# Casting loads for most of block 0, one-hot rows copied by engines, bounds from three products, and a new order table, in a fused attention and softplus kernel

## The chip, the cores and the metric

The kernel runs on one core of a Trainium2 chip. The metric is the device time of one execution in microseconds (us). Engines are named as in the profile: PE is the matrix engine, DVE the vector engine, ACT the scalar engine, POOL the GpSimd engine, SP the engine whose queue issues transfers. POOL issues transfers too.

## The reference

Two layers. The first is attention over 4 batches, 8 heads, 768 positions, 64 dimensions, in which each query sees only six chunks of 32 keys: those with the largest upper bound on the score.

```
k_min = min of k over each chunk of 32;  k_max = max
ub   = sum over d of max(q * k_min, q * k_max)        # one bound per query and chunk
ub   = where(query chunk >= key chunk, ub, -1e9)
top  = the 6 chunks with the largest ub
scores = q @ k.T / 8, kept where the chunk is in top and the key is not later than the query
attn = softmax(scores) @ v
```

The second layer takes the 3072 rows of attn (512 wide): `h = x @ w_in` (512 x 2048), `g = max(h, 0) + log1p(exp(-|h|))`, that is ln(1 + exp(h)), and `out = g @ w_out` (2048 x 512). Inputs and output are float32.

## The kernel before

The work is cut into 12 blocks: 4 batches by 3 stretches of 256 queries. For each block n the program makes operations with short names, which the order table and this text use:

- `ld k n`, `ld q n`, `ld v n`: loads into a bfloat16 buffer (tile io; v for values), two for each, `.0` and `.1`. For n > 0 they are casting transfers (float32 in memory, bfloat16 on chip) that POOL issues. For block 0 q and k come as float32 by SP's queue into tile wx (`load_pairs`), in halves of four heads, and an operation `cast` on ACT or DVE makes bfloat16 of each.
- `kT`, `qT`: transposes on PE (with the matrix ident), for blocks 0 to 2; later blocks use transposing transfers `kD`, `qD`.
- `kx`, `kn`: maxima and negated minima of k by chunk (DVE, two reductions). `bd`: these, copied into a block-diagonal tile BD. `kc`: keys copied into tiles ka and kb. `qc`: queries copied into tile qt; `qac`: a second copy into tile qa.
- `qpn`: the positive part of q and the positive part of -q (tiles qpos, qneg). `ub`: products of these with BD, which give the bound, and for blocks 0 to 2 a product with constants (rows4, neg4) that puts later chunks out.
- `mx`: the largest six (DVE); `raw`: which chunks are out; `mT`: that matrix transposed on PE (blocks 0 to 2), or by a transfer `mD` (later); `mc`: the result copied under q, so that the score product adds a large negative number to what is out. For this the key tiles hold one-hot rows: `oh` makes them, `ohk` are transfers on SP's queue that put them into ka and kb.
- `s`: scores (PE); `ex`: exp (ACT); `af`: the causal edge (POOL); `av`: the product with v (PE); `nm`: division (DVE); `oT`, `xc`: transpose and copy into x (blocks 0 to 2), `xD` later.
- `h`: eight matmuls with w_in for two of 16 column tiles of the second layer; `e`, `ln`: exp and ln(1 + .) on ACT; `y`: products with w_out; `ye`: eviction; `st`: the store.

Block 0 does its attention's front end in two groups of four heads (g0, g1), so `kT0`, `kx0`, `mx0` and the like occur twice or more.

Nothing is scheduled at run time. A string, ORDER, names every operation once, with a letter for the engine (P, A, V, G, S for PE, ACT, DVE, POOL, SP) and `#i` for the i-th operation of that name. Each engine runs its operations in that order, and one waits for what it depends on and for free buffers. A word `z12` puts matmuls on a zero tile there, worth 12 units of 128 columns: four units make one matmul of 512 columns, the rest are matmuls of 128. They compute nothing that is used; this text calls them dummies.

Of the kernel before, what the change touches and what calls it, by code (L numbers as in the profile page):

```python
# [12 lines left out]
ALU = mybir.AluOpType  # L13
# [7 lines left out]
NP = H // 2  # L21
# [124 lines left out]
def dve(n, rate=1.0):  # L146
# [47 lines left out]
    sizes=dict(s=2, h=2, y=1, o=1, t=2, xp=4, kT=2, io=8, kx=2, q=2, pn=1, ub=2, pt=4, osw=2, x=3, g=2, e=3, ysb=4,  # L194
# [7 lines left out]
Vzero Sld_k0.0 Acast_k0.0 Vmr0#1 Vkb0 Vmr0 Gvone Gident z32 PkT0 PkT0 Sld_q0.0 Vr4 Gc4 Vbd0 Vkx0 Vkn0 Sld_k0.1  # L202
Vcast_k0.1 Acast_q0.0 z6 PqT0 PqT0 Aqc0 Vbd0#2 Gld_k1.0 Gld_k1.1 Vqpn0 Aqpn0 Sld_q0.1 Acast_q0.1 z36 PqT0 Gld_q1.0
Gld_q1.1 PkT1 Vcm0 Voh Akc0 Akc0 PkT0 PkT0 Sohk Sohk#3 Sohk PqT0 Vkx0 Vkn0 Aqc0 Aqpn0#3 z5 PkT1 Pub0 Gld_q2.0 Aqpn0
Akc0#3 Vmx0 Vraw0 Gqac0#1 Gbd0#3 Gqac0 Gld_v0.0 Gld_v0.1 Vkx1 Sohk z28 PmT0 PqT1 PqT1 Amc0 Aqc1 Vkn1 Vbd1 Vkc1 z16
Ps0#2 z5 Pub0 Ps0 Vmx0 Vqpn1 Vraw0 z35 PmT0 Vqac1 Amc0 Aqpn1 Pub1 Aex0#2 Aex0 Akc0 Vmc0#3 Gld_k2.0 Gld_k2.1 Vmc0 z7
Ps0#4 Ps0 Aex0 Gld_q2.1 Gld_v1.0 Aex0#4 Gld_v1.1 Gaf0 z12 Ps0#5 Aex0#5 Vmx1 Vraw1 z3 Ps0 Gaf0 Aex0 Pav0 z3 Pav0 Gaf0
Gw_in0 Vnm0 Gaf0 PqT2 Gw_in1 Gld_q3.0 Ps0#7 PmT1 Vmc1 Gw_in2 Akc1 z4 PoT0 Ps0 Aex0 Aex0 z12 Ps1#12 Pav0 Pav0 Aex1#12
Axc0 PkT2 PkT2 Ps1#4 Vmc1 Gaf0#6 Gaf0 Gaf0 Aex1#4 Vnm0 Gaf0 Gld_k3.0 z3 PqT2 Ps1#5 Aex1#5 PoT0 z1 Ps1#7 z5 Ps1 Gcm z10
Pav0#6 Pav0#7 Gvone Vkx2 Vkn2 Vnm0#3 Axc0 Aqc2 Aex1#7 Aex1 z7 Ps1 Aex1 z3 Pav0 Vbd2 Vqpn2 Vqpn2 Ps1#3 Aex1#3 Gaf1#1  # L210
PoT0#3 z1 Ps1 z4 Ps1#15 Pav0 Vnm0 Vkc2 Vqac2 Aex1 Gaf1 z4 Ps1#8 Pub2 Axc0#3 Aex1#15 Ps1#11 Aex1#8 Aex1#11 Gw_in3 PoT0
Ps1#13 Pav1 z3 Ps1#9 Pav1 Gld_k3.1 Aex1#13 Gw_out0 Gaf1#6 Gaf1 Ps1#14 Axc0 Vmx2 Gaf1#7 Vraw2 Aex1#9 Aex1#14 Ph0 Ps1#10
Aex1#10 Ps1 Vnm1 Gaf1 Aex1 Ae0 Gaf1 Gld_q3.1 PmT2 Vmc2 Ph0 Gaf1 Pav1#6 Pav1#7 Vnm1#3 Vkc2 Ps2#6 Ae0 Gld_v2.0 Aex2#6
Ps2#8 Aex2#8 Ph0#3 Aln0 Ps2#2 Pav1 Pav1 Ps2 Aex2 Ph0 SkD3 Vnm1 Vmc2 Ps2#12 Pav1 Pav1 Aex2#2 PoT1 Vxc1 Ae0 Vnm1 Ps2#5
Vbd0 PoT1 Ph0 Aex2#12 Aex2#5 Ae0 Ps2#17 PoT1 Ps2#14 Aex2#17 Vxc1 Vxc1 Ph0 PoT1 Vxc1 Ps2 Aex2#14 Ae0 Ps2#9 Ae0 Aex2 Ph0
Ps2#11 Aex2#9 Gaf2 Aex2#11 Ae0 Gw_out1 Ph0 Ae0 Ps2 Ps2 Gaf2#4 Gaf2#2 Ph1 Gaf2#5 Ph1#2 Gld_v2.1 Vkx3 Aex2 Aex2 Ps2#18
Aln0 Gaf2 Pav2 Ps2 Gwh0 Gw_out2 Vkn3 Vbd3 Gw_out3 Aex2#18 Py0 Aex2 Ae1 Ps2 Aln0 Aex2 Ps2#22 Ph1 Ae1 Aex2#22 Gld_k4.0
Gld_k4.1 Gld_k5.0 Gwh2 Ae1 Gld_q4.0 Py0 Ps2 Gaf2 SqD3 Ph1#5 Gld_q4.1 Aln1 Ps2#20 Pav2 Ph1#4 Aex2#20 Ps2 Vnm2 Gld_k5.1
Pav2 Ae1#4 Aex2 PoT2 Ae1#5 Axc2 Pav2 Aln0 Aex2 Vqpn3 Vqpn3 Pub3 Vuba3 Vkc3 Vnm2 Vmx3 Ph1 Ph1 Ps2 Aex2 Ae1 Aln1 Vqac3
Vraw3 Py0 Pav2 Pav2 Ps2#21 Vwv0 Vkc3 Ae1 Ps2#23 Aex2#23 Py0 Gaf2#7 Aye0 Ph1 Ps2 Vwv6 SmD3 Gwh4#1 Gwh2 Gaf2 Aex2#21 Ae1  # L220
Aln1 Aex2 SkD4 Sohk Gwd2 Vnm2 Vwv2 Py0 Py0 Py0 Py0 PoT2 PoT2 Aye0 Vxc2 Axc2 Aln1 Pav2 Pav2 SqD4 Py1 Py1 Py1 Sohk Skb0
Gld_v3.0 Vnm2 PoT2 Gld_q5.0 Amc3 Ps3#2 Aex3#2 Ps3#6 Aex3#6 Vkx4 Gld_q5.1 Vkn4 Vxc2 Vwh6#1 Py1 Aqpn4 Ps3#4 Ps3 Ph2
Vqpn4 Vbd4 Vkc4 Pub4 Vmc3 Gld_v3.1 Vuba4 Aye1 Vmx4 Vraw4 Vqac4 Ae2 Ph2 Aex3#4 Aex3 Ph2 Ps3#7 Ps3 Py1 Gaf3#4 Gld_k6.0
Gaf3 Gaf3#2 Ae2 Aln2 Aex3 SkD5 Aex3#7 SmD4 Ae2 Gaf3 Vkx5 Ph2#4 Gld_k6.1 Ps3#5 Ps3 SqD5 Vkc4 Aex3 Aex3 Ae2#4 Ph2#5
Ae2#5 Vkn5 Aln2#2 Py1 Pav3 Pav3 Vnm3 Gaf3#6 Gaf3#7 Gld_q6.0 Gaf3#5 Gld_q6.1 Gld_v4.0 Gaf3 Gld_v4.1 Ph2 Vmc4 Pav3#6
Pav3#7 Py1 Vnm3#3 Ae2 Ps4 Ps4#8 Ps4#4 Aln2 Ps4#9 Pav3#4 Pav3#5 Ph2 SkD6 Aex4#4 Vmc4 Aex4 Aex4#8 Aex4#9 Vnm3#2 Ps4 Ae2
Aex4 Vbd5 Vqpn5 Vqpn5 Py1 Pav3 Pav3 Ps4#3 Pub5 Aex4#3 Aye1 Ps4 Ps4#11 Aex4#11 Gaf4#5 Ph2 Vnm3 Ps4#15 Ps4 Py2 Vuba5
Vmx5 Vraw5 Gld_v5.0 Py2 Aex4 Ps4#12 Gaf4#1 Gaf4 Ae2 Aln2 Vkx6 Aex4 Aex4#12 Aex4#15 Pav4 Ps4#7 Aex4#7 Py2 Ps4#14
Aex4#14 Gld_q7.0 SxD3 Ps4 Ps4 Ps4 Vqac5 Gld_k7.0 Ph3 Pav4 Vkc5#1 Aex4#10 Aex4#13 Sst1 Gaf4#4 Vkn6 Aex4 Ph3 Ae3 Ae3
Aln3 Pav4#4 Vkc5 Ph3#6 Pav4#5 Vnm4 Gld_k7.1 SmD5 Vmc5 Ps5#18 Gld_k9.0 Gaf4#6 Gld_v8.0 Gld_v5.1 SqD6 Gaf4#7 Gaf4 Sst0#1  # L230
SkD7 Ps5 Gld_k9.1 Gaf4 Ps5#19 Aex5#18 Aex5#19 Aex5 Py2 Vmc5 Ps5#23 Pav4#6 Ps5 Vnm4#2 Pav4#7 Vnm4#3 Ps5#4 Ps5 Ae3#6
Ph3#4 Aex5 Aex5#23 Aex5 Aex5#4 Pav4 Ps5#12 Ps5#20 Pav4 Aex5#12 Aex5#20 Ps5#6 Ps5#14 Aex5#6 Aex5#14 Ph3 Ps5#10 Ps5#21
Gld_q7.1 Gld_v7.0 Gaf5#7 Gaf5#6 Ps5#8 Ps5#22 Vwh0 Vye2 Vqpn6 Vqpn6 Py2 Vkc6#1 Vwd6 Vnm4 Vbd6 Vwv4 Ae3#4 Aex5#21 Aex5#8
Aex5#10 Ps5#9 Ph3#5 Ps5#11 Ae3 Pub6 Ph3#7 SxD4 Aex5#22 Gld_q9.0 Aex5#11 Ae3#5 Pav5#6 Ph3 Gaf5#3 Gaf5#4 Gaf5 Gaf5#2
# [813 lines left out]
```

## Time and profile before

| | |
|---|---|
| median of 3 timed runs | 255.87 us (255.48 to 256.6) |
| profiled execution, first to last instruction (its only time on the page) | 254.5 us |
| PE busy in it | 247.7 us (97%) |
| ACT, DVE, POOL busy | 212.2, 177.5, 119.6 us |
| matmuls, dummies among them | 2790, 86 |

PE's busy time counts dummies, and the ends of its matmuls are modelled, so 97% is no measure of useful work. Rows of a time line give the start, the time until the last of the run has ended, the engine, the line of the program, the output and inputs, the shapes and the number of instructions merged; in brackets stands idle time before it and what ended it.

### The profile page before, as it was taken

How to read it: one execution, taken by the hardware profiler on the slowest of the kernel's cores; microseconds unless marked ns; L12 is line 12 of the kernel's file. 1: busy time of each engine (PE TensorE's matmuls, PEld its weight loads, DVE VectorE, ACT ScalarE, POOL GpSimd, SP SyncE). 2: the span in 40 equal slices, each digit the busy share in tenths (PEclk: the TensorE clock that was granted, in tenths of full speed). 3: DMA queues.
4: the chain of work that ended last, by engine and by line, in shares of the span. 5: the costliest groups of instructions: out<-in, count | busy, mean ns of one | idle time of the engine just before them, and what ended most of it. 6: DMA issues, size and time to landing. Idle time of an engine off the chain costs nothing.

```text
span 254.5 us, 7076 instructions
## 1 busy us (share of the span) xinstructions
PE 247.7 (97%) x2790; PEld 202.7 (80%) x2790; DVE 177.5 (70%) x568; ACT 212.2 (83%) x389; POOL 119.6 (47%) x197
## 2 busy tenths in 40 slices
PE   8989989999999999999999999999999999999995
PEld 3557788786677788786789998989989988998864
DVE  5999876083999988667987998975784542656231
ACT  4959989997899999969798878998888999766561
POOL 6689857918494995758556640041030105101000
PEclk9999999999999999999999999999999999999999
DMA  6999999999999999999999995211032060020015
GB/s 170 147 133 129 193 195 193 162 164 152 138 130 145 188 157 135 142 172 194 159 146 158 100 119 168 43 24 36 8 85 62 3 206 3 1 85 3 0 58 193
DMA packets 113954, 29.90 MB, mean 117 GB/s; under 512 B 103776, under 2 KB 110944, under 8 KB 113920
## 3 DMA queue, kind: packets, MB, share of 16 engines
q0 software_dynamic: 74944, 13.11, 69.7%
q1 hardware_dynamic: 38976, 16.33, 32.9%
q8 instruction: 22, 0.36, 0.6%
q14 instruction: 12, 0.10, 0.1%
HBM read 27.26 MB, written 6.29 MB: 132 GB/s over the span
## 4 chain that ended last, share of the span: by engine, by line
PE 88%; DVE 8%; DMA 2%; issue 1%; ACT 0%; DVEq 0%
PE ph L895 31%; PE py L925 10%; PE pt L840 9%; PE py L840 8%; PE ps L696 6%; PE po L726 6%; PE ps L697 4%; PE py L1011 3%; DMA mT<-mraw 2%; PE ph L925 2%; PE pt L696 2%; DVE kx L507 2%; PE pt L726 2%; PE pt L579 2%; PE pt L697 1%; DVE qa L294 1%
## 5 line engine op out<-in xcount | busy, mean ns | idle before, releaser
L895 PE MATMUL ph<-x,w_in_sb 128*128 128x256 bf16 x768 | 97.9, 272 | 0.0
L704 ACT ACTIVATE pt<-ps 128x512 bf16<-128x512 f32 (+1 forms) x145 | 75.5, 550 | 9.3 <-PE ps L697 8.2
L714 POOL TENSOR_SCALAR_AFFINE_SELECT pt<-pt 128x256 bf16<-128x256 bf16 x96 | 40.7, 447 | 89.5 <-ACT pt L704 80.7
L895 PEld LDWEIGHTS <-w_in_sb 128*128 128x128 bf16 x768 | 72.4, 98 | 9.0
L900 ACT ACTIVATE e<-ph 128x512 f32<-128x512 f32 x96 | 57.0, 607 | 15.2 <-PE ph L895 15.0
L905 ACT ACTIVATE g<-e 128x1024 bf16<-128x1024 f32 x48 | 50.5, 1065 | 0.4
L925 PE MATMUL py<-w_out_sb,g 128*128 128x512 bf16 (+1 forms) x144 | 33.5, 367 | 0.0
L726 PEld LDWEIGHTS <-pt 128*128 128x128 bf16 x672 | 28.5, 97 | 2.6
L704 ACT ACTIVATE pt<-pt 128x512 bf16<-128x512 f32 (+1 forms) x47 | 26.3, 571 | 3.9 <-PE pt L697 3.1
L925 PEld LDWEIGHTS <-g 128*128 128x128 bf16 x176 | 16.4, 98 | 11.7
L726 PE MATMUL po<-v,pt 128*128 128x65 bf16 x516 | 24.4, 193 | 0.0
L840 PEld LDWEIGHTS <-g 128*128 128x128 bf16 x224 | 21.2, 98 | 2.6
L499 DVE TENSOR_REDUCE kx<-kT 128x32 bf16<-128x1024 bf16 x18 | 21.5, 1209 | 1.1 <-DMA kT<-io 1.0
L363 POOL DMA_DIRECT2D v<-in_v_dram x24 | 21.7, 908 | 0.0
L363 POOL DMA_DIRECT2D io<-in_k_dram x22 | 20.1, 921 | 0.0
L363 POOL DMA_DIRECT2D io<-in_q_dram x22 | 19.7, 901 | 0.1
L696 PE MATMUL ps<-qa,ka 96*128 96x256 bf16 x72 | 19.0, 273 | 0.7 <-DVE qa L294 0.6
L696 PE MATMUL ps<-qt,kb 128*128 128x256 bf16 x73 | 19.1, 272 | 0.0
L739 DVE RECIPROCAL rew<-po 128x4 f32<-128x4 f32 x38 | 6.7, 177 | 16.1 <-PE po L726 15.9
L840 PEld LDWEIGHTS <-df 128*128 128x128 bf16 x168 | 16.0, 98 | 2.0
L697 PE MATMUL ps<-qt,kb 128*128 128x256 bf16 (+1 forms) x73 | 17.3, 245 | 0.0
L740 DVE TENSOR_TENSOR osw<-po,rew 128x256 bf16<-128x256 f32 x38 | 16.1, 424 | 1.3
(134 smaller groups left out, 421.0 us busy)
## 6 DMA issues: line engine op xcount, KB each, us to landing
out_dram<-ysb SPq DMA_DIRECT2D x23, 256.0 KB, 2.6
v<-in_v_dram POOLq DMA_DIRECT2D x24, 128.0 KB, 5.7
io<-in_k_dram POOLq DMA_DIRECT2D x22, 128.0 KB, 6.0
io<-in_q_dram POOLq DMA_DIRECT2D x22, 128.0 KB, 6.1
w_in_sb<-in_moe_w_in_dram POOLq DMA_DIRECT2D x4, 512.0 KB, 7.2
w_out_sb<-in_moe_w_out_dram POOLq DMA_DIRECT2D x4, 512.0 KB, 7.4
wx<-in_k_dram SPq DMA_DIRECT2D x2, 256.0 KB, 3.8
wx<-in_q_dram SPq DMA_DIRECT2D x2, 256.0 KB, 4.0
```

Source lines behind the costliest of these rows:

```text
L363: lambda e, t=t: nc.gpsimd.dma_start(out=into(nm, n, t), in_=rows(nm, n, t)),
L499: nc.vector.tensor_reduce(kx.ap[:, :, j].rearrange("d p (t c) -> d t p c", t=NT), kT.ap.rearrange("d p x -> d (p x)").rearrange("d (t p c ...
L696: nc.tensor.matmul(sp.ap[:, 0:QB], kk[0:nr, p, j * 128:(j + 1) * 128], qq, start=True, stop=True)
L697: nc.tensor.matmul(sp.ap[:, QB:w], kk[0:nr, p, (j + 1) * 128:(j + 2) * 128], qq[:, 1] if last else qq, start=True, stop=True)
L704: lambda e, sp=sp, pt=pt, h=h, j=j, w=w: nc.scalar.activation(pt.ap[:, h, j:j + 2].rearrange("k j c -> k (j c)")[:, 0:w], sp.ap[:, 0:w], A ...
L714: nc.gpsimd.affine_select(out=d, in_=d, compare_op=ALU.is_ge, fill=0.0, base=0, channel_multiplier=-1, pattern=[[0, 2], [1, 128]])
L726: nc.tensor.matmul(o[:, u, h], pt.ap[:, h, j, c0:c0 + 128], T.V[i][:, j, 2 * p + h, :], start=(j == 0), stop=(j == t0 + u))
L840: nc.tensor.matmul(bank.ap[:, c * HD:(c + 1) * HD], a(f), w(f), start=start and f == 0, stop=f == HF - 1, skip_group_check=True)
L895: nc.tensor.matmul(o[:, j], T.w_in[:, dt, ft * 128:(ft + 1) * 128], x.ap[:, dt], start=(dt == 0), stop=(dt == KDM - 1))
L900: lambda e, hb=hb, eb=eb, f2=f2: nc.scalar.activation(eb.ap[:, f2 * 512:(f2 + 1) * 512], hb.ap, ACT.Exp),
L905: lambda e, eb=eb, g=g, f4=f4: nc.scalar.activation(g.ap[:, f4 * 4:(f4 + 1) * 4].rearrange("f j c -> f (j c)"), eb.ap, ACT.Ln, bias=1.0),
L925: nc.tensor.matmul(yb.ap[:, 0:c1 - c0], g.ap[:, f, u * 128:(u + 1) * 128], T.w_out[:, f, c0:c1], start=(f == 0), stop=(f == KFF - 1))
```

## The change

1. `load_pairs`: only the first half of k (`ld k0.0`) still comes as float32 through wx and a cast. The second half of k and both halves of q become casting transfers issued by POOL. The io tile of block 0 is filled in another layout (head, then position), so that each transposition takes one head (64 columns in, 64 rows out) and not a pair.
2. The one-hot rows of the first 256 keys are copied into ka and kb by an engine (`ohc`; ACT in the new table) instead of by two transfers on SP's queue.
3. For blocks 0 to 2, `qpn` makes the part of -q only. `ub` uses q times the maxima, plus the positive part of -q times both: three products where two were.
4. `bd`, `qac` and `qpn` of blocks 0 to 2 may now run on POOL.
5. The sums of w_out that reuse wx wait for one cast and not for four, and tile wx is lent to one load.
6. ORDER is replaced as a whole. Two lines of it, before and after, where the transposition of block 2's mask stands (`PmT2`):

```diff
 ORDER = """
...
-PoT0#3 z1 Ps1 z4 Ps1#15 Pav0 Vnm0 Vkc2 Vqac2 Aex1 Gaf1 z4 Ps1#8 Pub2 Axc0#3 Aex1#15 Ps1#11 Aex1#8 Aex1#11 Gw_in3 PoT0
-Aex1#10 Ps1 Vnm1 Gaf1 Aex1 Ae0 Gaf1 Gld_q3.1 PmT2 Vmc2 Ph0 Gaf1 Pav1#6 Pav1#7 Vnm1#3 Vkc2 Ps2#6 Ae0 Gld_v2.0 Aex2#6
+Aex1 Ae0#2 Ph0 Ps1#14 Aex1#14 Ae0 Pub2 Ps1 Ps1 Aex1#3 Aex1 Vkc2#1 Vkc2 Vmx2 Vcm0 Vraw2 Gw_out1 Gld_q3.0 Gld_q4.0
+Gaf1#6 Gld_k3.1 Ph0 Ae0 Ps1#15 Aex1#15 Ph0 Ae0 Ps1#10 PmT2 Ps1 Aex1 Ph0 Aln0 Ae0 Aex1 Vmc2 Gld_v2.0 Gld_q3.1 Gaf1#2
...
     for k0, k1 in ((0, 1), (1, NBLK)):
         for h in range(2):
-            o = P.op("ohk", [("SP", 450)], lambda e, k0=k0, k1=k1, h=h: rows_of(0, k0, k1, h), [oh],
-                     key=par["ohd"][k0] * 1e3, dma=300 if k0 == 0 else 750)
+            if k0 == 0:
+                o = P.op("ohc", [("DVE", 400), ("ACT", act(1024, False)), ("POOL", 1150)], lambda e, h=h: copy(
+                    e, (T.KB[0][32:64] if h else T.KA[0][64:96])[:, :, 0:QB],
+                    T.ohb[:, 0:QB].unsqueeze(1).to_broadcast([32, NP, QB])), [oh], key=3000)
...
+            if nm == "k" and g == 0:
+                st = Buf(pool["xp"])
+                d = P.op(f"ld {nm}{n}.{g}", [("SP", 560)], lambda e, st=st, x=rows_in: nc.sync.dma_start(
+                    out=st.ap.rearrange("s h t d -> s h (t d)"), in_=x()), key=1e3 * when[g], dma=950, alloc=[st])
...
+            else:
+                o = P.op(f"ld {nm}{n}.{g}", [("POOL", 890)], lambda e, x=rows_in, out=out: nc.gpsimd.dma_start(
+                    out=out(), in_=x()), key=1e3 * when[g], dma=750, touch=[SBt[nm, n]] if first else [], **new)
...
+                    if pairs:
+                        for h in range(2):
+                            nc.tensor.transpose(o[h * D:(h + 1) * D, p - p0, t * 128:(t + 1) * 128], x[:, 2 * p + h, t], T.ident)
+                        continue
...
-            for j in range(2):
+            for j in (1,) if bound else (0, 1):
...
-                        for j in range(2):
-                            nc.tensor.matmul(o[:, (p - p0) // 2, t, p % 2], split(qpn.ap[j])[:, p, t],
-                                             T.BD[i][:, p, j, :, 0:C], start=(j == 0), stop=(j == 1 and not bound))
+                        parts = [(qpn.ap[0], 0), (qpn.ap[1], 1)]
+                        if bound:
+                            parts = [(qab.ap[1], 0), (qpn.ap[1], 0), (qpn.ap[1], 1)]
+                        for x, (qq, j) in enumerate(parts):
+                            nc.tensor.matmul(o[:, (p - p0) // 2, t, p % 2], split(qq)[:, p, t],
+                                             T.BD[i][:, p, j, :, 0:C], start=(x == 0), stop=(j == 1 and not bound))
```

How the change moves work shows on three engines. The first is POOL, around the loads of blocks 0 and 1 and the first loads of w_in (io_97 to io_100 hold blocks 1 and 2; in the new program io_95 and io_96 are block 0's q and k). Before:

```order
L317 AFFINE_SELECT neg_68<-neg_68 128x4
L363 DMA io_97<-in_k_dram 128x8x64 x2
L363 DMA io_98<-in_q_dram 128x8x64 x2
...
L714 AFFINE_SELECT pt_113<-pt_113 128x2x128
L391 DMA w_in_sb<-in_moe_w_in_dram 128x4x512
L714 AFFINE_SELECT pt_113<-pt_113 128x2x128
```

Now:

```order
L398 DMA io_95<-in_q_dram 128x4x128
L398 DMA io_96<-in_k_dram 128x4x128
L398 DMA io_95<-in_q_dram 128x4x128
L368 DMA io_97<-in_k_dram 128x8x64 x2
L368 DMA io_98<-in_q_dram 128x8x64
...
L409 DMA w_in_sb<-in_moe_w_in_dram 128x4x512
L368 DMA v_70<-in_v_dram 128x8x64
L409 DMA w_in_sb<-in_moe_w_in_dram 128x4x512
L294 COPY bd_76<-kx_104 64x8x8 x2
```

Three loads of block 0 have come to the head of POOL's queue, and the first two of w_in's four loads have moved ahead of the first causal edges (AFFINE_SELECT on pt), with thirteen smaller loads in front of the first.

The second is DVE, from its first reduction of keys (kx_103 is block 0, kx_104 block 1). Before:

```order
L507 TENSOR_REDUCE kx_103<-ph_87 128x2x8 x2
L294 CAST io_95<-wx 128x4x2x64
L294 COPY bd_76<-kx_103 64x4x8 x2
L560 TENSOR_SCALAR qpos_109<-qt_106 128x512
L309 MEMSET cmask 128x4
L305 SCALAR_TENSOR_TENSOR ohb<-ident 32x768
L507 TENSOR_REDUCE kx_103<-ph_88 128x2x8 x2
```

Now:

```order
L305 SCALAR_TENSOR_TENSOR ohb<-ident 32x768
L327 MEMSET kb_74 32x1536
L324 MEMSET bd_76 128x192
L323 MEMSET mraw_78 128x256
L314 MEMSET neg_68 128x4
L315 COPY rows_67<-ident 128x128
L294 CAST io_96<-wx 128x512
L531 TENSOR_REDUCE kx_103<-ph_87 128x2x8
L294 COPY qt_106<-ph_88 128x512
L323 MEMSET mraw_79 128x256
L531 TENSOR_REDUCE kx_103<-ph_87 128x2x8
```

The one-hot rows, a memset and the only cast now stand ahead of the first reduction, and a copy of q stands between the two reductions of group g0.

The third is ACT, from its last exponentials of block 0 (written into pt, read from ps) to its first of block 1. Before:

```order
L293 COPY kb_74<-pt_92 64x4x256
L704 ACTIVATE pt_116<-ps_85 128x384
L704 ACTIVATE pt_116<-ps_86 128x384
L704 ACTIVATE pt_114<-ps_85 128x512
L293 COPY x_121<-pt_91 128x256
```

Now:

```order
L732 ACTIVATE pt_116<-ps_85 128x384
L732 ACTIVATE pt_116<-ps_86 128x384
L293 COPY qa_107<-ph_88 32x2x256 x2
L293 COPY qt_108<-ph_88 32x2x256 x2
L732 ACTIVATE pt_113<-ps_85 128x512
```

Four copies of block 1's mask (`mc1`, into qa_107 and qt_108) have moved from DVE to ACT, between the exponentials of block 0 and those of block 1.

## Rows read from the trace of the kernel before

**Rows 1.** The page's first line.

```profile
span 254.5 us, 7076 instructions
```

**Rows 2.** Busy time by stretch (PE, PEld, DVE, ACT, POOL), granted clock, transfer share, GB/s.

```profile
30.00:40.00 10.00, 9.22 (x129) 8.24 (x128) 8.11 (x30) 8.67 (x19) 5.77 (x11) 1.00 1.72 188
40.00:60.00 20.00, 20.00 (x226) 15.97 (x225) 10.13 (x34) 19.53 (x36) 13.64 (x19) 1.00 1.56 165
100.00:200.00 100.00, 99.38 (x1173) 85.78 (x1172) 78.04 (x258) 87.56 (x162) 41.91 (x69) 1.00 0.92 106
```

**Rows 3.** Groups of PE instructions by line: the dummies.

```profile
L1011 PE MATMUL py<-zero 128*128 128x512 bf16 x53 | 15.9, 417 | 1.1 <-DVE zero L303 1.1
L1013 PE MATMUL py<-zero 128*128 128x128 bf16 x33 | 4.3, 218 | 0.0
```

**Rows 4.** Time line of PE, 1 to 33 us.

```profile
1.06 3.59 PE L1011 MATMUL py<-zero 128*128 128x512 bf16 x8 [1.06 <-DVE zero L303]
4.53 0.60 PE L480 MATMUL ph<-ident,io 128*128 128x128 bf16 x4
...
5.60 2.11 PE L1011 MATMUL py<-zero 128*128 128x512 bf16 x9
...
13.64 1.89 PE L1011 MATMUL py<-zero 128*128 128x512 bf16 x8
15.37 0.33 PE L1013 MATMUL py<-zero 128*128 128x128 bf16 x3
...
17.12 0.19 PE L579 MATMUL pt<-bd,qpos 128*128 128x32 bf16 x1
...
17.74 0.38 PE L1011 MATMUL py<-zero 128*128 128x512 bf16 x1
...
30.42 1.03 PE L895 MATMUL ph<-x,w_in_sb 128*128 128x256 bf16 x8
31.30 0.27 PE L696 MATMUL ps<-qt,kb 128*128 128x256 bf16 x1
...
32.67 0.40 PE L642 MATMUL pt<-ident,mraw 128*128 128x128 bf16 x4 [0.78 <-DVE rew L739]
```

**Rows 5.** Time line of DVE, 5 to 38 us.

```profile
5.17 1.29 DVE L507 TENSOR_REDUCE kx<-ph 128x16 bf16<-128x512 bf16 x2 [1.67 <-PE ph L480]
6.40 0.90 DVE L294 CAST io<-wx 128x512 bf16<-128x512 f32 x1
...
8.17 0.94 DVE L305 SCALAR_TENSOR_TENSOR ohb<-ident 32x768 bf16<-32x768 bf16 x1
...
13.29 0.81 DVE L294 COPY bd<-kx 64x64 bf16<-64x64 bf16 x2
...
21.04 0.85 DVE L294 COPY qa<-ph 32x512 bf16<-32x512 bf16 x2
...
26.60 0.43 DVE L560 TENSOR_SCALAR qpos<-qt 128x1024 bf16<-128x1024 bf16 x1
...
28.48 0.67 DVE L294 COPY ka<-pt 64x1024 bf16<-64x1024 bf16 x1
...
38.10 0.29 DVE L294 COPY x<-pt 128x256 bf16<-128x256 bf16 x1 [0.30 <-PE pt L757]
```

**Rows 6.** Time line of ACT, 3 to 14 us.

```profile
3.85 0.62 ACT L293 CAST io<-wx 128x512 bf16<-128x512 f32 x1 [1.76 <-DMA wx<-in_k_dram]
...
13.15 0.58 ACT L293 COPY qt<-pt 32x512 bf16<-32x512 bf16 x1
```

**Rows 7.** Time line of POOL, 1 to 8 us.

```profile
1.30 0.29 POOL masks.py:199 TENSOR_SCALAR_AFFINE_SELECT ident<-ident 128x128 bf16<-128x128 bf16 x1
...
5.29 2.63 POOL L363 DMA_DIRECT2D io<-in_q_dram x3
```

**Rows 8.** Transfers of the first 40 us: size, median us from issue to landing.

```profile
w_in_sb<-in_moe_w_in_dram POOLq DMA_DIRECT2D x4, 512.0 KB, 7.2
...
io<-in_q_dram POOLq DMA_DIRECT2D x6, 128.0 KB, 4.7
```

## What the change should do to the time

> **What bounds the kernel now.** I read the stretches first. From 40 us on PE is never seen idle for long: 20.00 of 20 us between 40 and 60, 99.38 of 100 between 100 and 200 [rows 2]. So there each microsecond of matmul work put in or taken out is a microsecond of time, and a gain elsewhere counts only if it lets PE do its work earlier. Then the groups of PE by line: 53 dummies of 512 columns and 33 of 128 [rows 3]. All stand in the first 30 us of the program. They, and waits, are the only part of PE's time that can go without taking work out. Then the time line of PE [rows 4], for three points. The first transposes start at 4.53 us, behind eight dummies. The first group of h, the filler of the whole middle, starts at 30.42. The transposes of block 2's mask, at 32.67, are the last that PE waits for in the open (0.78 us, for DVE); from there on attention and the second layer overlap. Last the time line of DVE [rows 5], since it is DVE's chain from the first reduction of keys (5.17) to block 2's mask that sets 32.67.
>
> So I forecast in two steps: how much of the old work PE has behind it when it comes to block 2's mask, and when it comes there. What follows that point is old work and runs without waits that the trace shows.
>
> **Work ahead of block 2's mask.** Counted in the two order tables, priced by rows.
>
> Dummies: 245 units of 128 columns before (4 x 53 + 33), 187 in the new table (38 of 512, 35 of 128), all ahead of this point. Eight of 512 start at 13.64 and the next matmul at 15.37 [rows 4]: 0.216 each, 0.054 a unit. So 58 fewer are -3.1 us.
>
> Added matmuls: block 0's k and q need 32 transposes for 16; each has 128 columns, as a unit has: 16 x 0.054 = +0.9. The bounds of blocks 0 to 2 get a third product, 8 for each block: 24 more. 24 such matmuls run from 17.12 to 17.74 [rows 4], 0.026 each: +0.6. Together +1.5, all ahead of this point.
>
> Old work pulled ahead: four groups of h stand ahead of the mask's transposes, where one stood. A group takes 0.88 (30.42 to 31.30 [rows 4]): +2.6. One pass of scores of 384 to 512 columns has gone behind it: -0.2. So have two value products, 14 matmuls of 65 columns, by the rate of the dummies an estimate of 0.4: -0.4. Net +2.0. If PE comes to the mask at 32.67 as before, it has 2.0 us less left, and the program ends 2.0 earlier.
>
> All in all PE has 0.4 more to do ahead of this point (-3.1 + 1.5 + 2.0). The 0.78 that it waited there covers that, if DVE is no later.
>
> **When DVE has block 2's mask.** Start of the chain: 14 dummies stand ahead of the first transposes, where eight stood. Eight take from 1.06 to 4.53, 0.43 each, half of the later rate (nine from 5.60 need 2.11 with the drain, 0.22 to 0.23 each [rows 4]); 0.216 is the rate of the full level of 2.4 GHz, 0.43 that of 1.2, though the granted clock reads 1.00 in all stretches shown [rows 2]. Six more end at 5.8 if all are fast, at 7.1 if all are slow; PE was slow at 4.53 and fast by 5.60, so I take a change at 5.0 and an end at 6.1. Eight transposes more (0.45) and the first reduction starts at 6.6, against 5.17: +1.4 (bounds +1.1 and +2.4). DVE's new work ahead of it is covered by those dummies: one-hot rows 0.94 and the cast 0.90 [rows 5] are the most of it, with three memsets and a copy; begun when ident is ready (1.59 [rows 7]) it ends at about 5.5.
>
> Taken off DVE between there and the mask [rows 5]: a cast 0.90, the one-hot rows 0.94, block 1's bd 0.81 (to POOL), two mask copies of block 1, 0.85 each, and one of block 0, half of that (to ACT), a relu of block 2 0.43, its qac at the same size (to POOL): 5.6. Put on it: three copies into x at 0.29, the second copy of block 2's keys 0.67, a copy of block 2's q from PSUM, as large, 0.67; two qac and a bd of block 0 (were POOL's), 0.9 by half the sizes in the rows; a memset of 0.27 by estimate; a copy of q of block 0, 128x512 from PSUM, which no row shows: at least a reduction over as much (0.64), at most the cast (0.90); I take 0.65, as it has the reduction's size and source. Sum 4.0. Net -1.6 against +1.4: 0.2 earlier.
>
> Against that stands POOL, which now issues loads almost without a pause from 1.6 to about 16 us: 13 loads at 0.88 (2.63 for three [rows 7]), then w_in. DVE's cast at 6.40, beside such an issue, took 0.90, ACT's of the same shape 0.62 [rows 6]. I add 0.5 for DVE's small copies there (bounds 0 and 1.5). That puts the mask at 33.0, 0.3 later than now. The first group of h then comes 5.8 earlier (4 groups, 7 passes, 32 products), at 27.2, against 30.42.
>
> The one-hot copies cost nothing: two copies on ACT while it has no other input (its first cast was at 3.85 [rows 6]). The 0.58 per mask copy that ACT takes over [rows 6], four times 0.58, lies ahead of block 1's exponentials, in the wait for the same point.
>
> **Sum.** -2.0 for work pulled ahead, +0.3 for the mask: -1.7. The profiled span is 254.5 [rows 1], 1.4 below the median of the timed runs, 255.87; I take the change off the median: **254.1 us**. Bounds: the mask at 32.2 (no collisions, an early start) or at 34.6 (a late one, all collisions); and, since the whole order is new, the 0.6 us that PE is not busy between 100 and 200 [rows 2] gone or doubled. That gives 252.7 to 256.5: 254.1 less 0.8 and 0.6, and 254.1 plus 1.6 and 0.6, rounded.
>
> **A rule against the change.** DVE and POOL collide in the rows above, and DVE pays: its cast was 0.90, while POOL's three issues beside it stayed at 0.88 each [rows 5, 7]. The Trainium skill ("SBUF — State Buffer", section "SBUF: two separate sides", box on the "DVE blocks DMA" trap) says that it goes the other way too: while DVE holds the port it shares with GpSimd, GpSimd cannot write descriptors, and loads from its queue stand still. No run here shows that.
>
> **Rivals.**
> *The casting loads come late.* Mechanism: POOL's first loads wait until DVE's opening work ends at 5.5. The second half of k, second in the queue, would then be issued from 6.4 and land 4.7 later [rows 8], at 11.1. DVE's reduction of it is due at 8.8, transposes 0.45 ahead of it: 8.3. So 2.8 late, and 256.9. Undisturbed it is issued at 2.5 and lands at 7.2: 1.1 in hand. For: POOL's queue now carries what SP's did, behind nothing but ident. Against: POOL's issues at 5.29 ran beside DVE work at full pace [rows 5, 7]. [...]
>
> *ACT takes the lead back.* ACT is busy 8.67 of 10 us from 30 to 40 and 19.53 of 20 from 40 to 60 [rows 2], so PE's lead holds only if ACT comes earlier too. It can win 1.3 + 0.5 us there; if it wins half, 0.9, the time is 255.0. For: the new table gives ACT mask copies right before block 1. Against: it also loses casts and relus.
>
> *Slower: the first weights come late.* The first group of h needs the second load of w_in, POOL's 16th load. Fifteen issues of 0.88 behind 1.6, with 0.6 for a select and a memset by estimate, send it out at 15.4; it lands 7.2 later [rows 8], at 22.6, 4.6 us ahead of its use at 27.2. Behind 2.9 MB at 165 GB/s [rows 2] (18 us from 2.5 on) it is no later. Each microsecond past 27.2 costs one; from 30.2 on the kernel is slower by over 0.5%. If it lands at 31: 257.9.
>
> **Chances.** Half a per cent (254.6 and 257.15) is about what this measurement can tell from no change. Forecast, with its spread, ends faster: 0.52. ACT takes it back: 0.20, same. Loads late: 0.16, same but for 0.02. Weights late or another new wait of that size: 0.12, of which 0.10 slower. So faster 0.52, same 0.36, slower 0.12. The range 252.7 to 256.5 leaves out most of the weights' case, half of the loads' and little below: under 2 in 10.
>
> **What would show it.** Right: dummies of about 10 us in place of 13; the first reduction at 6.6, the first h near 27, block 2's mask transposed near 33 with four groups of h ahead of it, no wait of PE over 1 us behind it. Wrong: transposes of the second half of k that wait for a transfer; h's first matmul released by a load of w_in; or PE gaps after 40 us that [rows 2] do not have, which would mean that the new order lost later what it won at the start.

## The result: slower, by one part in ninety

| | before | changed |
|---|---|---|
| median of the timed runs | 256.19 us (4 runs) | 258.97 us (4 runs) |
| ratio, 95% interval | | 1.0115 (1.0073 to 1.0156) |
| span of the profiled execution | 254.5 us [rows 1] | 257.1 us |
| last matmul ends | 251.45 us | 252.95 us |
| from there to the span's end | 3.05 us | 4.15 us |

The forecast was 254.1 us, with a range from 252.7 to 256.5. The time lies outside it, on the other side of the kernel before. The profile of the changed kernel, by the views that were used on the old one. First the page's span, then busy time by stretch (PE, PEld, DVE, ACT, POOL, granted clock, transfer share, GB/s) and the two groups of dummies:

```profile
span 257.1 us, 7127 instructions
```

```profile
30.00:40.00 10.00, 10.00 (x151) 8.95 (x149) 7.24 (x32) 9.93 (x20) 7.74 (x14) 1.00 1.92 177
40.00:60.00 20.00, 19.98 (x214) 14.99 (x213) 11.03 (x37) 18.14 (x35) 10.29 (x15) 1.00 1.73 168
100.00:200.00 100.00, 98.61 (x1158) 85.67 (x1156) 80.25 (x269) 87.09 (x161) 39.56 (x71) 1.00 0.76 106
```

```profile
L1038 PE MATMUL py<-zero 128*128 128x512 bf16 x38 | 13.7, 473 | 1.1 <-DVE zero L303 1.1
L1040 PE MATMUL py<-zero 128*128 128x128 bf16 x35 | 4.4, 219 | 0.0
```

The wait for block 2's mask is gone: PE is busy 10.00 of 10 us from 30 to 40, where it was 9.22 [rows 2]. But between 100 and 200 us it is idle 1.39, where it was 0.62. So something that the old order had hidden now shows behind the start.

The time line of PE has the points that the forecast named (first transposes, first mask transposes, first group of h, block 2's mask):

```profile
1.06 6.15 PE L1038 MATMUL py<-zero 128*128 128x512 bf16 x14 [1.06 <-DVE zero L303]
7.15 0.41 PE L501 MATMUL ph<-ident,io 128*64 128x128 bf16 x8
7.49 0.34 PE L1040 MATMUL py<-zero 128*128 128x128 bf16 x3
...
13.81 0.41 PE L664 MATMUL pt<-ident,mraw 128*64 128x128 bf16 x4 [0.80 <-DVE mraw L652]
...
28.55 1.04 PE L922 MATMUL ph<-x,w_in_sb 128*128 128x256 bf16 x8
...
34.16 0.39 PE L670 MATMUL pt<-ident,mraw 128*128 128x128 bf16 x4
```

The fourteen dummies took 0.43 each up to the last: none ran at the fast rate that the old kernel's had reached by 5.6 [rows 4]. They held PE to 7.15, though the cast that the transposes read had ended at 5.3. DVE's first reduction began at 7.60, not at 6.6:

```profile
4.52 0.78 DVE L294 CAST io<-wx 128x512 bf16<-128x512 f32 x1
7.60 0.69 DVE L531 TENSOR_REDUCE kx<-ph 128x16 bf16<-128x512 bf16 x1 [2.31 <-PE ph L501]
```

The first group of h begins 1.9 earlier than before, the mask 1.5 later.

From the mask's transposes to PE's last matmul the old program took 251.45 - 32.67 = 218.8 us. The new one takes 252.95 - 34.16 = 218.8. By the forecast it should have taken 2.0 less, since that much of the old work stands ahead of the mask now. PE did that work early and lost as much time behind it, in waits. Here are two of the places, and what DVE did ahead of each:

```profile
105.61 1.05 PE L922 MATMUL ph<-x,w_in_sb 128*128 128x256 bf16 x8 [0.76 <-DMA x<-osw]
124.09 0.27 PE L724 MATMUL ps<-qa,ka 96*128 96x256 bf16 x1 [0.63 <-DVE qa L294]
```

```profile
97.03 0.43 DVE L585 TENSOR_SCALAR qpos<-qt 128x1024 bf16<-128x1024 bf16 x1 [1.21 <-DMA qt<-io]
...
99.33 0.17 DVE L767 RECIPROCAL rew<-po 128x4 f32<-128x4 f32 x1
...
120.72 1.48 DVE L294 COPY bd<-kx 64x64 bf16<-64x64 bf16 x2
```

At 105.61 h of block 4 waits for the transfer of x. The division (99.33) that this transfer needs stood behind block 6's relus, which waited for a transposing load of 8.8 us. At 124.09 the scores of block 7 wait for a mask copy that stood behind two reductions and a `bd` that took 1.48 us; one further on took 0.36.

To follow a lead through the program I use one number from the trace's records: the start of a matmul, less the matmul work done before it (a column per 1/2.4 ns and 2 ns for each matmul, 25 ns at least, dummies left out). It grows by each wait, each dummy and each slow stretch. A smaller number is a lead. The rows are us of work done; the last two are the end and all work. The columns beside the first two are experiments told below whose traces hold all matmuls. (That of oldorder2 holds them too; it ends with a lead of about 1.0 on the kernel before. In those of loads, late5, late5w and late6 some are missing.) Each column is one execution.

```
work     before    after     tail    xd_m7     warm oldorder    prods   prods2
   16     20.82    18.66    17.37    18.33    17.35    19.09    19.02    18.56
   32     21.05    19.27    18.54    18.93    19.16    19.29    21.55    18.70
   56     21.18    19.88    18.94    19.65    20.07    19.50    21.67    19.31
   80     21.51    20.39    19.46    20.16    20.58    19.91    22.01    19.65
  104     22.62    22.43    21.56    21.48    22.97    20.98    22.19    19.83
  160     22.96    22.84    21.97    21.89    23.37    21.25    22.58    20.37
end       23.44    23.44    22.58    22.49    23.98    22.29    23.06    20.85
all      228.01   229.51   229.51   229.51   229.51   229.51   228.62   228.62
```

Shortly behind the mask (16 us of work) the changed kernel is 2.16 us ahead. At the end it is 0.00 ahead, and by this count it has 1.50 more work. With 1.10 more behind the last matmul that is 2.6, the difference of the spans.

### The profile page after: what moved, and what is told of

Its sections match the earlier page's. It is cut to its first block, busy times and chain, and to the rows that moved or that the text cites. A ratio compares the mean times of both kernels' runs of the same rounds, so it can differ in the third digit from the quotient of the medians.

```text
span 257.1 us, 7127 instructions
## 1 busy us (share of the span) xinstructions
PE 248.6 (97%) x2817; PEld 202.4 (79%) x2817; DVE 181.2 (70%) x573; ACT 210.7 (82%) x381; POOL 120.9 (47%) x198
## 4 chain that ended last, share of the span: by engine, by line
PE 74%; DVE 13%; DMA 6%; ACT 2%; issue 1%; SPq 0%; POOL 0%; DVEq 0%; ACTq 0%
PE ph L922 27%; PE pt L867 10%; PE py L867 7%; PE py L952 7%; PE ps L724 5%; PE po L754 4%; PE ps L725 4%; DMA qt<-io 3%; PE py L1038 3%; DVE ub L634 2%; DVE kx L523 2%; PE pt L754 2%; DMA mT<-mraw 1%; DMA out_dram<-ysb 1%; PE pt L724 1%
## 5 line engine op out<-in xcount | busy, mean ns | idle before, releaser
L732 ACT ACTIVATE pt<-ps 128x384 bf16<-128x384 f32 (+1 forms) x147 | 75.8, 553 | 7.3 <-PE ps L725 6.6
L952 PE MATMUL py<-w_out_sb,g 128*128 128x512 bf16 x144 | 36.0, 379 | 0.0
L732 ACT ACTIVATE pt<-pt 128x512 bf16<-128x512 f32 (+1 forms) x45 | 25.1, 567 | 2.1 <-PE pt L725 1.3
L952 PEld LDWEIGHTS <-g 128*128 128x128 bf16 x176 | 16.1, 97 | 11.1 <-ACT g L932 0.2
L867 PEld LDWEIGHTS <-g 128*128 128x128 bf16 x224 | 20.9, 98 | 2.4
L725 PE MATMUL ps<-qa,ka 96*128 96x256 bf16 (+1 forms) x74 | 17.4, 243 | 0.0
```

Of the source, the lines that this page charges most:

```text
L725: nc.tensor.matmul(sp.ap[:, QB:w], kk[0:nr, p, (j + 1) * 128:(j + 2) * 128], qq[:, 1] if last else qq, start=True, stop=True)
L732: lambda e, sp=sp, pt=pt, h=h, j=j, w=w: nc.scalar.activation(pt.ap[:, h, j:j + 2].rearrange("k j c -> k (j c)")[:, 0:w], sp.ap[:, 0:w], A ...
L867: nc.tensor.matmul(bank.ap[:, c * HD:(c + 1) * HD], a(f), w(f), start=start and f == 0, stop=f == HF - 1, skip_group_check=True)
L952: nc.tensor.matmul(yb.ap[:, 0:c1 - c0], g.ap[:, f, u * 128:(u + 1) * 128], T.w_out[:, f, c0:c1], start=(f == 0), stop=(f == KFF - 1))
```

## The experiments

All were timed in turns with the kernel before on one chip; ratios are to it, with a 95% interval. What the letters and names of the order table mean stands above.

**1. tail: the last store.** In the changed kernel the last tiles' stores bunch at 251.4 to 253.4 us, behind a DVE operation that stands behind an eviction.

```diff
-Vye11 Vyf10 Sst10#1
+Vyf10 Vye11 Sst10#1
```

> One word of the new order moves: block 10's last sum (yf10, on DVE) goes ahead of block 11's first eviction (ye11), behind which it waited for PE although its inputs were there; the two stores of block 10 behind it can leave some 3 us earlier. Theory A (the new order puts ready work behind waiting work, late in the program): the last store no longer shares the transfer engines with three others, the stretch from the last matmul to the end falls from 4.2 us to about 3.1, and the time from 258.97 to about 257.9. Theory B (the loss is made at the start, by the loads through POOL and the added work; late places only show it): the end of the span moves by less than 0.3 us, 258.7 to 259.3.

258.41 us, 1.0097 (1.0066 to 1.0129): closer to B. The stores are spread now, and from the last matmul to the end it takes 4.2 us, as before the edit: that theory falls. But the profile gave something else. This execution has the changed kernel's instructions up to 246 us, word for word, and its dummies turned fast at about 4.8:

```profile
1.06 5.03 PE L1038 MATMUL py<-zero 128*128 128x512 bf16 x14 [1.06 <-DVE zero L303]
6.03 0.41 PE L501 MATMUL ph<-ident,io 128*64 128x128 bf16 x8
...
47.78 1.02 PE L952 MATMUL py<-w_out_sb,g 128*128 128x512 bf16 x4 [0.48 <-DMA w_out_sb<-in_moe_w_out_dram]
...
106.15 1.02 PE L952 MATMUL py<-w_out_sb,g 128*128 128x512 bf16 x4 [0.98 <-DVE ysb L294]
```

So it began its transposes 1.12 us earlier, and of that 0.87 reached the last matmul. New waits at 47.8 (for w_out) and 106.2 took some back.

**2. xd_m7: the two waits shown above.**

```diff
-Vkc7 Vnm4 Vuba6
+Vkc7 Vuba6
-Vkn6 Vqpn6 Vqpn6 Vbd6
+Vkn6 Vnm4 Vqpn6 Vqpn6 Vbd6
-SkD8 SxD4 Sst0
+SxD4 SkD8 Sst0
-Vkn9 Vbd9 Vmc7#1 Vbd8 Vmc7
+Vkn9 Vmc7#1 Vmc7 Vbd9 Vbd8
```

> Two places of the new order are undone where PE stood still after 100 us. Block 4's last division (nm4) goes ahead of block 6's relus on DVE, which wait for a transposing transfer, and on SP's queue block 4's x (xD4) goes ahead of block 8's keys (kD8); and block 7's mask copies (mc7) go ahead of two bd copies on DVE. Theory A: PE's gaps of 0.92 before h at 105.6 and 0.79 before scores at 124.1 both close, nothing behind them opens, and the time falls by 1.4 to 1.7, to about 257.4. Theory B: PE reaches those places early only to wait for something else (ACT, the next mask); the gaps reappear within 20 us and the time stays within 0.5 of 258.97.

258.16 us, 1.0092 (1.0061 to 1.0123): between the two. Both waits are gone (1.4 us by the brackets above, 1.7 from start to start by the records), and this one of PE (second row) has come, behind a DVE that waited for a store to free its tile:

```profile
104.83 0.69 DVE L294 COPY ysb<-py 128x512 f32<-128x512 f32 x1 [3.04 <-DMA out_dram<-ysb]
```

```profile
113.03 0.19 PE L607 MATMUL pt<-bd,qneg 128*128 128x32 bf16 x1 [0.88 <-DVE qneg L583]
```

**3. warm: fewer dummies ahead of the first transposes.**

```diff
-z56 PkT0
+z40 PkT0
```

> The first run of dummies is cut from 14 to 10 matmuls; nothing else changes. In the profile the 14 ran at half rate throughout (0.435 us each) and ended at 7.15, while DVE's cast of k had ended at 5.3. Theory A (the start is late because of the dummies themselves): the first transposes start at 5.4 to 5.5, the first reduction of keys at 5.9 instead of 7.6, and block 2's mask is transposed 1 to 1.5 us earlier than 34.16; the time falls by 1 to 1.5, to 257.5 to 258.0. Rival C (DVE's chain after that waits for loads by POOL or for ACT): the first reduction comes earlier but block 2's mask by less than 0.4, and the time stays within 0.4 of 258.97. Were the clock to rise later for it, transposes and short matmuls would run at half rate for longer, and the gain would shrink by as much.

258.83 us, 1.0113 (1.0082 to 1.0143): C. The transposes start at 5.36 and the first scores at 12.39 (14.88 in the changed kernel). At 48 us that lead meets the last quarter of w_out, at 107 a store:

```profile
48.39 1.02 PE L952 MATMUL py<-w_out_sb,g 128*128 128x512 bf16 x4 [1.11 <-DMA w_out_sb<-in_moe_w_out_dram]
...
107.55 1.02 PE L952 MATMUL py<-w_out_sb,g 128*128 128x512 bf16 x4 [1.27 <-DVE ysb L294]
```

In the table above, warm starts 1.3 ahead of the changed kernel and ends 0.5 behind it. (This execution took 259.28 us, more than the median.) The new order multiplies by w_out from 39.5 us on, the old one from 45.8. In these rows a start made earlier only brings PE to these transfers sooner. No run issues the last load of w_out earlier in the new order, so whether the lead would then hold is not shown.

**4. oldorder: all code edits, the old order.** Its words are changed only where operations have come, gone or moved to another engine, as here:

```diff
-Vzero Sld_k0.0 Acast_k0.0 Vmr0#1 Vkb0 Vmr0 Gvone Gident z32
+Vzero Sld_k0.0 Gident Gld_q0.0 Voh Acast_k0.0 Gld_k0.1 Gld_q0.1 Aohc Aohc Vmr0#1 Vkb0 Vmr0 Gvone z32
-Vqpn0 Aqpn0 Sld_q0.1 Acast_q0.1 z36
+Aqpn0 z36
```

> All edits to the code, with the order table of the kernel before, changed only where operations are gone or new: three loads of block 0 go to the head of POOL's queue, the casts and four relus go, the one-hot rows are made first on DVE and copied by ACT behind its cast. Theory A (the edits cost little, the new order costs most): added work +1.5 on PE, DVE relieved of a cast and of the one-hot rows in its chain; 256.2 to 257.5, below the changed kernel by 1.5 or more. Theory B (the edits themselves cost the time): 258.5 or more.

257.49 us, 1.0063 (1.003 to 1.0096): at the upper bound of A. The twelve runs fall into two groups, six from 256.1 to 256.9 and six from 258.0 to 259.7, and the trace is of one of the first group (256.94); it does not show what delays the others. By the ratios about half of the loss goes with the new order, though the interval overlaps that of the changed kernel (1.0073 to 1.0156). What is left in this trace is the added 1.50 of work against a lead of 1.15 at the end, and 0.4 behind the last matmul.

**5 and 6. late5 and late5w: all late places at once.** xd_m7 and tail, and besides the two stores of the first blocks ahead of the transposes that made them late:

```diff
-SxD4 SkD8 Sst0 Sst1#1
+Sst0 Sst1#1 SxD4 SkD8
-Sst11#1 Sst11
+Sst11 Sst11#1
```

> The changed kernel with five places of its order mended: the three of xd_m7, the tail's copy, on SP the two stores of blocks 0 and 1 ahead of the transposes that wait for block 4's result, and the last tile's full row stored before its half row. Theory A (the waits of 100 to 125 us and the late last store are the loss behind 40 us): the waits of 0.92 and 0.79 us close, the one of 1.03 at 113 us in xd_m7 does not open because the two stores issue at about 92 us and no longer at 100.6, and the last store lands 1.7 us after its issue and not 2.4: 256.2 to 257.0 us. Rival B (the waits open again elsewhere): 257.8 us or more.

> late5 with four of the fourteen dummies ahead of the first transposes left out. Theory C (a lead made at the start is lost where the last quarter of the second weights lands, about 48 us): first scores 1.5 to 2.5 us earlier than in late5 but the same time within 0.5 us, with a wait of 1 us or more for those weights near 48 us. Rival D (the start sets the end once the later waits are closed): 1.5 us or more below late5.

262.86 us, 1.0248 (1.0211 to 1.0285), and 262.99 us, 1.0264 (1.0224 to 1.0305): B, and worse than B. PE's waits in late5:

```profile
110.46 0.27 PE L724 MATMUL ps<-qa,ka 96*128 96x256 bf16 x1 [1.25 <-DVE qa L294]
116.20 0.18 PE L607 MATMUL pt<-bd,qpos 128*128 128x32 bf16 x1 [2.34 <-DVE osw L768]
117.26 0.21 PE L607 MATMUL pt<-bd,qneg 128*128 128x32 bf16 x1 [0.88 <-DVE qneg L583]
...
117.68 1.87 PE L922 MATMUL ph<-x,w_in_sb 128*128 128x256 bf16 x8
...
120.82 1.04 PE L922 MATMUL ph<-x,w_in_sb 128*128 128x256 bf16 x8
```

The waits are not all of it. Behind them PE's matmuls ran at half their rate: eight of h took 1.87 us at 117.68 and 1.04 at 120.82. With the four of y between them they took 3.14 us, where 1.74 would do at the full rate, so about 1.4 went there. The granted clock (the figure behind POOL's) fell to 0.72:

```profile
115.00:120.00 5.00, 2.70 (x25) 1.98 (x27) 4.67 (x28) 0.35 (x1) 0.00 (x0) 0.72 0.52 91
```

Of late5's six runs four have a mean granted clock of 0.990 to 0.993; in late6 below, no run is under 0.996. The reason for the waits shows in the transfers of 94 to 110 us (queue: packets, MB, share of 16 engines; then median us to landing), first of xd_m7, then of late5:

```profile
q0 software_dynamic: 8206, 1.03, 107.4%
...
kT<-io SPq DMA_TRANSPOSE x2, 5.8
```

```profile
q0 software_dynamic: 9838, 1.24, 130.2%
...
kT<-io SPq DMA_TRANSPOSE x1, 9.4
```

The two stores, issued at 91 us and not at 101, run beside the loads that POOL issues from 90 to 97. The loads' queue moves more after 94 (1.24 MB against 1.03), and the transpose of block 8's keys lands in 9.4 us. late5w had fewer dummies, but as late5's had turned fast early it started only 0.5 us ahead (first transposes at 5.35 and 5.88), so C and D stay untested by it. It waited 2.60 us for w_out at 50.70, the longest wait for those weights in any run.

**7. late6: late5 without the move of the two stores.**

> late5 without the move of the two stores: the changed kernel with the edits of xd_m7 and of tail, and the last tile's full row stored before its half row. Theory A (the two stores issued at 91 us are what made late5 slow, because they and the loads of 90 to 97 us share the DMA engines): close to xd_m7, 257.3 to 258.3 us, the transpose of block 8's K landing in under 7 us where late5 took 9.4. Rival B (it was another of late5's edits or their sum): 260 us or more. The last store, issued about 252 us, lands 2.4 us later as in after, since late5's took 2.7 with the same edit.

258.27 us, 1.0079 (1.0047 to 1.011): A. The same transpose lands in 6.1 us. It was the two stores: nothing else differs. The last store, with its rows swapped, landed 2.3 us after its issue: that idea falls too.

**8. loads: the code edits without the three products.** oldorder with two relus and two products again.

```diff
-            for j in (1,) if bound else (0, 1):
+            for j in (0, 1):
...
-                        if bound:
-                            parts = [(qab.ap[1], 0), (qpn.ap[1], 0), (qpn.ap[1], 1)]
```

> oldorder with the bounds formed from two products and two relus again, so that only the loads, the half transposes and the one-hot copies of the change are left. Theory A (what the code edits cost is the work they add on TensorE): TensorE's work 228.9 us (0.6 below oldorder), time about 256.9 us. Rival E (the relus taken off the vector and scalar engines pay for the added products at the start): 257.5 us or more, the first scores later than oldorder's 14.24 us.

258.23 us, 1.0079 (1.0052 to 1.0107): E by its time. It has less work than oldorder and is not faster. Its first scores come at 14.20, no later than oldorder's, so what the relus cost shows behind them. The wait for block 2's mask is back, and a wait behind DVE at 91 us with it. A third, at 9.13, is for block 1's keys, whose load stands behind three loads of block 0 in POOL's queue:

```profile
9.13 0.40 PE L503 MATMUL pt<-ident,io 128*128 128x128 bf16 x4 [0.69 <-DMA io<-in_k_dram]
...
33.59 0.40 PE L668 MATMUL pt<-ident,mraw 128*128 128x128 bf16 x4 [0.77 <-DVE rew L765]
...
91.16 0.27 PE L722 MATMUL ps<-qa,ka 96*128 96x256 bf16 x1 [0.97 <-DVE qa L294]
```

So the casting loads give nothing at the mask: it comes 0.9 later than in the old kernel [rows 4]. Their sixteen transposes and the wait at 9.13 are enough for that; no run takes the two apart.

**9. prods: the three products alone.** The kernel before, with one relu and three products for the bounds of blocks 0 to 2; four relus leave the old order, and nothing else is changed.

```diff
-            for j in range(2):
+            for j in (1,) if bound else (0, 1):
...
-                        for j in range(2):
+                        parts = [(qpn.ap[0], 0), (qpn.ap[1], 1)]
+                        if bound:
+                            parts = [(qab.ap[1], 0), (qpn.ap[1], 0), (qpn.ap[1], 1)]
+                        for x, (qq, j) in enumerate(parts):
```

> The kernel before with one part of the change alone: the bounds of blocks 0 to 2 from three products and one relu (four relus of the order go), float32 loads, casts, full transposes and one-hot rows by DMA as before. TensorE's work grows by 24 products of 0.026 us, 0.6 us. Theory A (oldorder's lead of 1.7 us at 16 us of work done, against none in loads, comes from the relus taken off the vector and scalar engines, and the old order keeps most of it): the wait of 0.94 us for block 2's mask shrinks below 0.3 us and the time is 255.2 to 256.0 us. Rival B (the lead comes from the loads and the products together, the relus alone give none): 256.6 us or more, the wait for the mask still 0.8 us or more.

255.47 us, 0.9979 (0.9948 to 1.001): A. No wait for the mask is left (its transposes start at 31.54), and the lead of 1.80 at 16 us of work is about oldorder's 1.73. But the profiled execution (256.5 us) loses all of it, most at two transfers:

```profile
47.53 1.02 PE L928 MATMUL py<-w_out_sb,g 128*128 128x512 bf16 x4 [0.54 <-DMA w_out_sb<-in_moe_w_out_dram]
...
51.51 0.37 PE L729 MATMUL po<-v,pt 128*128 128x65 bf16 x7 [1.54 <-DMA v<-in_v_dram]
```

The v is issued at 40.30, behind masking operations for which POOL waits, and lands 11.2 us later.

**10 and 11. prods2 and oldorder2: those two transfers earlier.** In both kernels:

```diff
-Gld_v2.0 Gaf2 Gw_out1 Gaf2#4 Gaf2#2 Gaf2#5 Gld_v2.1
+Gld_v2.0 Gw_out1 Gld_v2.1 Gaf2 Gaf2#4 Gaf2#2 Gaf2#5
```

(POOL's words alone; those of other engines stand between them.)

> prods with two loads issued earlier by GpSimd: the second quarter of w_out and the second half of block 2's V go right behind the first half of that V (about 34.3 and 35.1 us, in prods 36.8 and 40.3), ahead of four masking operations that wait for the scalar engine. Theory A (a lead made at the start is lost only where these two transfers land late; their landing varies by execution and spreads the times of prods over 254.4 to 256.5 us): the waits of 0.70 us at 47.5 and 1.70 us at 51.5 us go, the span is about 252.6 us and the time 254.2 to 254.9 us with less spread. Rival B (the transfers only push each other, w_out's other quarters or the transposes behind them come later): 255.4 us or more, a wait of 0.5 us or more at another place between 40 and 70 us.

> oldorder with the same two loads issued earlier. Theory A: the spread of 256.1 to 259.7 us closes towards its low end, 256.0 to 256.8 us: level with the kernel before, because 1.5 us of added work stands against about 1.1 us of lead. Rival B: 257.3 us or more.

prods2: 254.85 us, 0.9931 (0.9908 to 0.9953): A, and the only kernel here that is faster than the kernel before by more than its interval. POOL issues the two at 33.8 and 34.6, and PE waits for neither:

```profile
33.81 0.76 POOL L398 DMA_DIRECT2D w_out_sb<-in_moe_w_out_dram  x1
34.55 0.90 POOL L363 DMA_DIRECT2D v<-in_v_dram  x1
```

```profile
span 252.5 us, 7121 instructions
```

Here the lead of 2.26 at 16 us of work grows to 2.59 at the end, and 0.61 of work was added: the last matmul ends 1.98 earlier than in the old kernel, and the span is 2.0 shorter.

oldorder2: 257.5 us, 1.0027 (0.9998 to 1.0056): B by its median. The ratio is lower than oldorder's and its interval takes in 1, as A has it, so the two theories are not told apart. Its waits near 50 us are not to be seen, as they were not in oldorder's profile, and a wait of 0.85 us for DVE's mask copy at 89.57 has come, at the place where loads waited. So what delays half of oldorder's runs is not shown to be the two transfers.

## Why the prediction was wrong

The forecast took 1.7 us off the time; the spans differ by 2.6 the other way. Of the 4.3 between, 1.2 is the mask's time, 2.0 the work pulled ahead that bought nothing, and 1.1 the end.

**Work and dummies: right in the main.** 58 units fewer were to be 3.1 us, the added matmuls 1.5. Counted at the full rate, dummies went from 13.26 to 10.13 us (-3.13) and work from 228.01 to 229.51 (+1.50). Four groups of h stand ahead of block 2's mask, as counted. One price was too high. The new transposes use 64 of the 128 columns each (128*64 in their rows), and in the records two of them start together, 0.003 us apart: eight take 0.35 us (7.15 to 7.49), where four of the old ones take 0.23 (5.37 to 5.60, where dummies follow [rows 4]). So the sixteen more cost about 0.5 us, or 0.8 with the longer step from a dummy to them (0.15 for 0.06), and not 0.9. The old kernel's row:

```profile
5.37 0.40 PE L480 MATMUL ph<-ident,io 128*128 128x128 bf16 x4
```

**The mask's time: 34.16, not 33.0.** Nearly all of the 1.2 is in the first term: fourteen dummies ended at 7.15, past even the bound of 7.1 for all of them slow, where I took 6.1. The row showed a change of rate near 5.0 in one execution, and I took that for a time of the program. In xd_m7, with the same first instructions, the dummies ended at 6.94, in tail at 6.03. The later stations of the chain (7.60 for 6.6, 34.16 for 33.0) are late by the same amount, so the estimates of DVE's work between them held together, the 0.5 for collisions among them, which no run tests by itself. But the experiments show that this error was not what made the kernel slower: warm took four of the slow dummies out, started its transposes 1.8 us earlier and gained nothing.

**The step that failed: "what follows that point is old work and runs without waits that the trace shows".** The -2.0 rested on it whole. It holds for the old order. The work is old, but its order is new on all engines and queues, and the same 218.8 us pass from the mask on. By the table it loses 0.86 more than the old order from 16 to 56 us of work, 0.93 more from 80 to 104, 0.37 in the rest: 2.16. In the first of these stretches no wait is long: by the records six of 0.05 to 0.22 us, five of them ahead of scores, make up 0.84 of what it loses there. The waits that show singly come of queues: a division behind a relu that waits for a transposing load, mask copies behind reductions, a store behind a transpose that waits. The bounds had "the 0.6 us gone or doubled" for that, and the stretch of 100 to 200 us does lose 0.77 more. Such gaps were also the last of the prediction's own signs of being wrong. What was missing in the sum is that the stretch from 36 us on loses as well, and that a lead is not carried through by itself: PE ahead of its transfers waits for them. The executions of the new order show it: the changed kernel loses 4.8 behind 16 us of work, tail and warm, 1.3 further ahead there, lose 5.2 and 6.6.

**The upper bound was added up wrong.** A late start (2.4 for 1.4) and all collisions (1.5 for 0.5) put the mask at 35.0, not at 34.6, and the range would have ended at 256.7. The measured time lies beyond that too.

**A term that was not in the sum: the end.** From the last matmul to the end 4.1 to 4.4 us pass in the profiled runs of the new order, 3.1 to 3.5 in those of the old one. The last store has the same size and the same copy ahead of it, and it lands later. Queues and issues of the last microseconds, first of the old kernel, then of the changed one (packets, MB, share; KB, us to landing):

```profile
q1 hardware_dynamic: 189, 0.16, 14.6%
...
out_dram<-ysb SPq DMA_DIRECT2D x1, 128.0 KB, 1.7
```

```profile
q1 hardware_dynamic: 293, 0.38, 22.0%
q14 instruction: 1, 0.01, 0.9%
...
out_dram<-ysb SPq DMA_DIRECT2D x1, 128.0 KB, 2.4
```

Neither the spacing of the stores (tail) nor their order (late6) changed that. The changed kernel's view has a transfer that the old one's lacks: 8 KB of the instruction queue. By the trace's records it runs from 254.45 to 255.13. All packets of the last store are done by 254.76 but eight of its 128, which run one after another from 255.13 on. So they stood behind that transfer. In all seven traces of the new order such a transfer starts about 1.0 us behind the issue of the last store; in the six of the old order the last one starts 4.3 to 5.4 us ahead of it. No run moved it by itself, and why the new order has it there is open. The landing is 0.75 of the 1.1 us. Most of the rest passes behind the landing: 1.3 us in every kernel with the new loads, in the old order too, and 1.0 in the others.

**The rivals.** Late casting loads: no for the changed kernel, where PE waits for none of block 0's loads. But the margin was small: where the start came earlier, PE waited 0.3 us for block 0's q (warm at 8.47, late6 at 8.67), and in the old order 0.5 to 0.7 for block 1's keys (loads, oldorder, oldorder2). POOL's issues went on beside DVE's opening work, of which these rows are the first two and the last:

```profile
1.41 0.95 DVE L305 SCALAR_TENSOR_TENSOR ohb<-ident 32x768 bf16<-32x768 bf16 x1 [0.41 <-POOL ident masks.py:199]
2.63 1.34 DVE L327 MEMSET kb<- 32x1536 uint32 x1 [0.27 <-issue]
...
4.52 0.78 DVE L294 CAST io<-wx 128x512 bf16<-128x512 f32 x1
```

```profile
1.50 0.93 POOL L398 DMA_DIRECT2D io<-in_q_dram  x1
2.42 0.75 POOL L398 DMA_DIRECT2D io<-in_k_dram  x1
3.16 0.75 POOL L398 DMA_DIRECT2D io<-in_q_dram  x1
3.89 2.06 POOL L368 DMA_DIRECT2D io<-in_k_dram  x2
```

Had POOL waited for all of that work, the second and third loads would have been issued from 5.3 on; they were issued at 2.42 and 3.16. The issue from 3.89, which ran beside a copy and the cast, was longer: 1.19 us by the records, 0.88 for the next one of its kind. The Trainium skill ("SBUF — State Buffer", section "SBUF: two separate sides", box on the "DVE blocks DMA" trap) has GpSimd locked out of writing descriptors while DVE runs an operation in a mode that takes both ports, and gives a float32 copy within SBUF as one that does. It does not say so of all DVE work, which the rival's mechanism needs, and the trace does not show it of the memset, beside which two issues took 0.75 each. Whether the longer issue is that trap, no run shows. ACT taking the lead back: no. ACT is busy 18.14 of 20 us from 40 to 60, less than before [rows 2], and behind 30 us no wait of PE over 0.2 us ends at it. Late first weights: not w_in, which landed in 8.8 us (7.2 before [rows 8]) and held nothing up. The mechanism was right, but for w_out, which the rival did not name: it is what the runs that started earlier met at 48 us.

**What each part is worth.** By the ratios: the three products alone 0.2% faster and within the interval of no change, 0.7% faster with two loads moved out of their way. The code edits without the products (the casting loads and the one-hot copies, which no run takes apart) 0.8% slower. All code edits in the old order 0.6% slower, 0.3% with the two loads moved, and there no change is within the interval. The new order on top brings it to 1.2%. The gain of the change lay in the part that I priced at +0.6 us of matmuls: the four relus that it takes off the chain to block 2's mask. I had only one of these, 0.43 us, in DVE's account.

## What to carry to other kernels

A lead made at the start is worth something only if what PE meets next is there earlier too. So look up, for each transfer that the later work needs, how long before its use it lands, and move its issue together with the lead: prods2, with two loads issued earlier, kept all of its 2.26 us, and prods lost its 1.80, most of it to those two. When an order table is replaced as a whole, "the later part is the same work" is no argument: list the waits of the old order that were hidden by less than a microsecond, and price their return. And a change of several parts is best judged part by part in the old order, where two of these parts had opposite signs.

## What the hardware showed that was not expected

The dummies' rate is no fixed time of the program. With the first instructions unchanged, matmuls of 512 columns went from 0.43 to 0.22 us each (1.2 and 2.4 GHz) at about 3.9 us in one execution (late6), at 4.8 in another (tail) and not before 6.6 (xd_m7) and 7.1 (the changed kernel) in two more (over five executions the same fourteen dummies ended, and the transposes began, at 5.58, 5.88, 6.03, 6.94 and 7.15), while PE did nothing but such matmuls from 1.06 us on; the granted clock reads 1.00 in all of them, so the profile's row does not show this step between the two levels. It did show a later one: 0.72 from 115 to 120 us of late5, where PE had stood still for 2.34 and 0.88 us and then ran at half its rate up to 120.6.

The transposing transfer of one block's keys, the same bytes each time, landed in 4.2 us (changed kernel), 5.8 (xd_m7), 6.1 (late6) and 9.4 (late5), beside different stores and loads; between the last two, two stores are all that differs. These two, of 256 KB each and moved some ten microseconds ahead, cost 4.6 us by the medians, about 1.4 of it in the profiled run by the fall of PE's rate.

A load of 8 KB of instructions can hold up data. In every trace in which it met the last store, the last eight of the store's 128 packets were done 0.7 to 0.9 us behind the others, and the store landed 2.3 to 2.7 us after its issue, against 1.7 where the two did not meet.
